# Sliding attention and dropless experts on one core: routing steps, weight sums and the first tiles' transposes put in another order

## The chip, the cores and the metric

The kernel runs on one NeuronCore of a Trainium2 chip. The metric is the device time of one execution in microseconds; the time before is 662.97 us, the median of three runs (662.25 to 666.29).

## The reference

The attention has 8 batches, 8 heads, 576 positions and head dimension 64, with an ALiBi bias and a causal window of 128. Its output, 4608 rows of 512, goes to a layer of 8 experts (512 to 1024 to 512): each row goes to the expert with the greatest logit and is weighted with that expert's probability.

```python
scores = scale * np.matmul(q, k.transpose(0, 1, 3, 2))
scores = np.where(mask, scores + bias[None], -1000000000.0)
attn = np.exp(scores - np.max(scores, axis=-1, keepdims=True))
attn = attn / (np.sum(attn, axis=-1, keepdims=True) + 1e-09)
x = (attn @ v).transpose(0, 2, 1, 3).reshape(B * S, H * D)

logits = x @ w_gate
expert_idx = np.argmax(logits, axis=1)
gate_w = softmax(logits)[np.arange(N), expert_idx]
h = np.maximum(x_sorted[lo:hi] @ w1[e], 0.0)     # per expert e
y_sorted[lo:hi] = h @ w2[e]
return gate_w[:, None] * y_sorted[inv_perm]
```

## The kernel before

The order of the work is written by hand: every engine gets its instructions in the order in which the program's text is run, and works them off in that order.

**Attention.** Two batches make a pair, and there are four pairs (bp 0 to 3). A unit is a pair and two heads, so there are 16 units, four to a pair. The loop over i (64 steps) goes through the units in four steps each (g 0 to 3). A unit's work is: scores for four groups of key blocks (L792, TensorE or PE), their exponentials on ScalarE (ACT, L801 and L811), a multiplication with the bias factors on VectorE (DVE, L805, called the probability multiply below), the products with v (values, L835), the sums of the probabilities (L874) that DVE adds up (L886), and copies of the output into xT (L854, L856). Scores run three or four groups ahead of the values.

**Routing.** When a pair's fourth unit is done, `behind(bp)` returns 16 lists of routing steps (ten for pair 2), and `some()` runs one list in each of the following steps of the loop: in g 0, 1 and 3 behind the step's values, in g 2 between the sums and the next scores. The steps are:

- `gate` (L894 on PE, L899 and L901 on DVE): logits and sums of the pair, in three parts; `turn` (L918, copied by ACT at L919) turns them into gsr
- `scale_a`, `scale_a2`, `scale_b`, `scale_b2`: L927 to L979 on DVE, from gsr to the logits, their maximum and the choice of expert
- `scale_c`: the exponential (L984, ACT), then L986 to L990 on DVE, whose last product is es, the scales of the rows; `count` is L996
- `scales_squared` (L1134): four matmuls that read es; ACT copies them to sq (L1142)
- `place` (L1005 and L1007 on PE, then L1009 to L1022), `place2` (L1028 to L1037), `ones_at` (L1046, L1052), `ones_at2` (L1061), `enlist` (L1071 on PE)
- rows of pair 0: `squares_turned` (rt, a DVE transpose, L1156), then ro: `squares_scaled` (a copy of sq, L1164, POOL) and `squares_out` (four stores on POOL's queue for a whole tile, L1175)
- rows of pairs 1 and 2: `row_turned` (four transposes on PE, L1105, and a copy by ACT, L1107), then `row_out` (a copy of es and the store, POOL, L1114 and L1119); `row` (rs) is both

In pair 2 `early_holes` (L1238 on PE, L1240 to L1242 on DVE) stands ahead of enlist. The gates, turns, head sums, row transposes and small products all take their output banks from one pool of two, `ps_m`, so each waits until the bank of the one before the last has been read.

**Queues.** SP's queue holds the loads of q, k and v for two units ahead; each waits, by a read of one probability (`no_earlier_than`), for the multiply of the next step. POOL's queue holds the stores of the rows and later the gathers.

**Weight sums.** The experts use Strassen's scheme with seven half-size products, for which sums of quarters of w1 are made on DVE (L533 to L536, eight additions of 128x512 for expert 0, `ws_tasks`). They are spread over the steps i = 48, 49, 54, 55, 58, 59, 62 and 63, ahead of the step's `some()`.

**First tiles.** Behind the attention, expert 0's four gathered tiles are scaled (L1364), turned (`to_columns`, L1378) and copied (L1379). The first two turns stand between the three gates of pair 3: turn, gate, turn, gate, gate. The experts' matmuls (`strassen1`, L1601, and `strassen2`, L1668) use six banks of their own, `pair(0)` to `pair(2)`; in their order pair 2 is needed from the fourth product on.

Of the kernel before, what the change touches and what calls it, by code (L numbers as in the profile page):

```python
# [8 lines left out]
F32 = mybir.dt.float32  # L9
# [7 lines left out]
P = 128  # L17
# [441 lines left out]
def kernel(  # L459
# [50 lines left out]
    with ExitStack() as fast:  # L510
# [377 lines left out]
        def gate(bp, c):  # L888
            if bp not in gs:
                gs[bp] = xp.tile([P, 2 * S], F32, name="gs", bufs=1)  # L890
            ps = ps_m.tile([P, 512], F32, name="m")
            c0, n = ((0, LQ), (LQ, LQ), (2 * LQ, P))[c]
            for hp in range(HP):
                nc.tensor.matmul(  # L894
                    ps[32 * hp : 32 * hp + 32, :n], lhsT=wgd[:, hp, :], rhs=xT[bp][:, hp, c0 : c0 + n],
                    start=True, stop=True,
                )
            if c < 2:
                nc.vector.tensor_tensor(gs[bp][:, c0 : c0 + n], ps[:, :n], sumT[bp][:, :LQ], op=ALU.add)  # L899
            else:  # L900
                nc.vector.tensor_tensor(  # L901
                    gs[bp][:, c0 : c0 + n].rearrange("p (b q) -> p b q", b=2),
                    ps[:, :n].rearrange("p (b q) -> p b q", b=2),
                    sumT[bp][:, None, LQ:].to_broadcast([P, 2, S - LQ]), op=ALU.add,
                )
# [460 lines left out]
        def to_columns(g, j):  # L1366
            n = g["n"]
            nm = "" if n == NJ else "1"
            if j == 0:
                g["xT"] = g["pool"].tile([P, DB, n * P], F32, name="xgT" + nm)  # L1370
            c0, m = (j // 2 * g["half"] + j % 2 * P, min(P, g["half"] - j % 2 * P)) if n == NJ else (0, P)
            to = g["xT"][:, :, c0 : c0 + m]
            xn = g["xn", j]
            if in_rows(g):
                xn = xn.rearrange("p h a f -> p (h a f)")
                tp = ps_m.tile([P, 512], F32, name="m")
                for db in range(DB):
                    nc.tensor.transpose(tp[:, db * P : (db + 1) * P], xn[:, db * P : (db + 1) * P], ident[:])  # L1378
                nc.scalar.copy(to, tp.rearrange("p (d q) -> p d q", d=DB)[:, :, :m])  # L1379
            else:  # L1380
                m = parts_of(g)
                nc.vector.transpose(to[:, :, : m * TQ].rearrange("p h (k j) -> p k h j", j=TQ), xn[:, :m])  # L1382
# [40 lines left out]
        def behind(bp):  # L1423

            g3 = [lambda k=k: gate(bp, k) for k in range(3)]
            t3 = [lambda k=k: turn(bp, k) for k in range(3)]
            rs = [lambda t=t: row(bp, t) for t in range(TPB)]
            a, a2, b, b2, c, n, q, p, p2, o, o2, e = (
                [lambda f=f: f(bp)] for f in (
                    scale_a, scale_a2, scale_b, scale_b2, scale_c, count, scales_squared, place, place2, ones_at,  # L1430
                    ones_at2, enlist,
                )
            )
            if bp == 0:
                rt = [lambda t=t: squares_turned(bp, t) for t in range(TPB)]
                ro = [
                    lambda t=t: (squares_scaled(bp, t), squares_out(bp, t, nc.gpsimd)) for t in range(TPB)
                ]
                return [g3[0:1], g3[1:2], g3[2:] + t3[0:1] + rt[0:1], t3[1:] + rt[1:3], a, a2, b, b2, c + n, rt[3:5],
                        q + p, p2 + rt[5:6] + ro[0:2], o + ro[2:4], o2 + ro[4:5], rt[6:8] + ro[5:7],  # L1440
                        e + rt[8:9] + ro[7:9]]
            rt, ro = ([lambda t=t, f=f: f(bp, t) for t in range(TPB)] for f in (row_turned, row_out))
            if bp == 1:
                return [g3[0:1], g3[1:2], g3[2:] + t3[0:1], t3[1:], a + rt[0:1], a2 + rt[1:2], b + rt[2:3],
                        b2 + rt[3:4], c + n, rt[4:5], p + ro[0:2], p2 + ro[2:5], o + rs[5:6], o2 + rs[6:7], rs[7:8],
                        e + rs[8:9]]
            return [g3, t3, a + a2, b + b2 + rt[0:1], c + n + rt[1:2], rt[2:4] + ro[0:2], p + p2 + ro[2:4] + rt[4:6],
                    o + o2 + ro[4:6] + rt[6:8], ro[6:8] + rs[8:9] + [early_holes], e + [early_table, lambda: gather(fixed[0], x_d[: 3 * 2 * S, :])]]

# [2 lines left out]
        def some():  # L1452
            if tasks:
                for f in tasks.pop(0):
                    f()
# [15 lines left out]
        for i in range(NG):  # L1471
# [30 lines left out]
            else:  # L1502
                values(u, 1, (6, 7, 8))
                finish(u, 1)
            if i in (48, 49, 54, 55, 58, 59, 62, 63):
                ws_tasks.pop(0)()
            if u == len(units) - 1 and g == 1:
                first = [t for _, t in prepare(fixed[0])]
                tasks.extend([[], first[0] + first[1][1:]])
            if g != 2:  # L1510
                some()
            if g in (1, 3):
                scores_to(ahead)
            if g == 3 and hp == HP - 1 and bp < BP - 1:
# [318 lines left out]
        while tasks:  # L1833
            some()
        g_of = [lambda k=k: gate(BP - 1, k) for k in range(3)]
        for f in first[1][:1] + g_of[:1] + first[2] + g_of[1:]:
            f()
        for i in range(len(groups)):
# [78 lines left out]
```

## Time and profile before

| what | us |
|---|---|
| runs, median (lowest to highest) | 662.97 (662.25 to 666.29) |
| the profiled execution, time of its own | 661.93 |
| its span, first to last instruction | 660.1 |
| TensorE busy | 630.1 |
| weight load busy (lies beside the matmuls) | 527.8 |
| VectorE busy | 366.1 |
| GpSimd (POOL) busy | 271.5 |
| ScalarE busy | 214.9 |

All times in rows are microseconds from the start of the span. A row of the order of time has the start, the length (of several instructions that follow each other, from the first start to the last end), the engine, the line, the operation with its tiles, the count, and in brackets the time for which the engine was idle before it and what ended that. The attention with its routing fills the first 163 us; the experts follow. Pair 0 is routed from some 45 to 83 us, pair 1 from 82 to 121, pair 2 from 123 to 153.

### The profile page before, as it was taken

The numbers are of one execution on the slowest core, as the hardware profiler recorded it, in microseconds if no ns is written. First come the engines' busy times: TensorE is split into PE (matmuls) and PEld (weight loads), VectorE is DVE, ScalarE is ACT, GpSimd is POOL, SyncE is SP. The second block draws the span as 40 slices with busy tenths as digits, with TensorE's granted clock in tenths as the row PEclk, the third lists the DMA queues.
The fourth block names the chain that finished last, engine by engine and source line by source line (L and its number), as shares of the span: only waits on it lengthen the run. The fifth ranks groups of instructions, "written<-read, shape, count | busy, mean of one in ns | idle before, by whom it ended". The sixth has DMA issues, their size and how long they took to land.

```text
span 660.1 us, 14485 instructions
## 1 busy us (share of the span) xinstructions
PE 630.1 (95%) x5824; PEld 527.8 (80%) x5824; DVE 366.1 (55%) x745; ACT 214.9 (33%) x493; POOL 271.5 (41%) x459
## 2 busy tenths in 40 slices
PE   6889999998999999999999999999999999999993
PEld 5768877687987888878878887889788978887883
DVE  3437968588798758436633761484247435643510
ACT  6858677585330331023002311320131123102310
POOL 8100664234032783566066525642662466030002
PEclk9999999999999999999999999999999999999998
DMA  9885999975258924673196419443924592376002
GB/s 265 246 214 146 254 282 284 329 245 151 95 134 302 347 57 148 218 290 90 74 306 210 153 46 312 159 149 114 322 90 143 188 303 44 127 244 224 0 1 74
DMA packets 54928, 121.81 MB, mean 185 GB/s; under 512 B 5777, under 2 KB 21297, under 8 KB 54850
## 3 DMA queue, kind: packets, MB, share of 16 engines
q1 hardware_dynamic: 43074, 92.51, 44.0%
q0 software_dynamic: 10624, 27.38, 13.1%
q8 instruction: 48, 0.79, 0.5%
q10 hardware_dynamic: 1152, 0.88, 0.4%
q14 instruction: 30, 0.25, 0.1%
HBM read 101.58 MB, written 19.63 MB: 184 GB/s over the span
## 4 chain that ended last, share of the span: by engine, by line
PE 57%; issue 9%; DVE 7%; POOL 1%; ACT 0%; POOLq 0%; DVEq 0%
PE pair0a L1668 4%; PE pair1b L1668 4%; PE pair1a L1668 4%; PE pair0b L1668 4%; PE pair1a L1601 4%; PE pair1b L1601 4%; PE pair0b L1601 4%; PE pair2b L1668 4%; PE pair2a L1668 4%; PE pair0a L1601 4%; PE pair2b L1601 3%; PE pair2a L1601 3%; PE pair0a L1726 2%; PE pair2a L1726 2%; PE pair0a L1709 1%
## 5 line engine op out<-in xcount | busy, mean ns | idle before, releaser
L1345 POOL DMA_INDIRECT xg<-x_rows,p_idx x121 | 128.3, 1061 | 33.7 <-issue 28.0
L1693 POOL DMA_INDIRECT out_dram<-zo,s_idx x38 | 43.4, 1141 | 173.3 <-DVE zo L1682 144.8
L805 DVE TENSOR_TENSOR pe<-pe,fac 128x512 f32<-128x512 f32 x64 | 43.6, 688 | 41.6 <-ACT pe L801 41.6
L792 PE MATMUL sp<-q_sb,k_sb 64*64 64x192 f32 (+2 forms) x1152 | 55.7, 320 | 7.8 <-DMA q_sb<-in_qT_dram 5.3
L835 PE MATMUL at<-pe,v_sb 64*64 64x192 f32 (+2 forms) x1408 | 55.1, 282 | 2.5 <-issue 1.4
L835 PEld LDWEIGHTS at<-pe,v_sb 64*64 64x64 f32 x1408 | 47.2, 134 | 8.5 <-issue 2.8
L792 PEld LDWEIGHTS sp<-q_sb,k_sb 64*64 64x64 f32 x1152 | 40.4, 136 | 16.5 <-issue 6.6
L801 ACT ACTIVATE pe<-sp 128x512 f32<-128x512 f32 x64 | 38.4, 599 | 30.2 <-issue 14.2
L811 ACT ACTIVATE pe<-sp,mid 128x128 f32<-128x128 f32 x128 | 40.0, 371 | 0.0
L1615 ACT ACTIVATE h<-h 128x512 f32<-128x512 f32 (+1 forms) x32 | 20.0, 624 | 38.9 <-DVE h L1614 38.9
L874 PE MATMUL m<-pe,ind 128*32 128x192 f32 (+2 forms) x576 | 25.6, 311 | 1.7 <-issue 1.0
L1543 POOL COPY paced_by<-h 1x1 f32<-1x1 f32 x47 | 18.5, 393 | 19.6 <-DVE h L1717 15.8
L1364 DVE TENSOR_TENSOR xn<-xg 128x512 f32<-128x512 f32 (+1 forms) x39 | 25.7, 662 | 1.3 <-DMA xg<-x_rows,p_idx 1.3
L874 PEld LDWEIGHTS m<-pe,ind 128*32 128x32 f32 x576 | 19.0, 109 | 6.7 <-issue 1.4
L1164 POOL COPY xs<-sq 128x16 f32<-128x16 f32 x6 | 1.7, 290 | 51.3 <-ACT sq L1142 51.3
L541 DVE TENSOR_TENSOR w2s<-w 128x512 f32<-128x512 f32 x16 | 10.9, 684 | 20.6 <-DMA w<-in_moe_w_dram 20.6
L1382 DVE STREAM_TRANSPOSE xgT<-xn 128x512 f32<-128x512 f32 (+1 forms) x31 | 21.7, 698 | 1.1
L854 ACT COPY xT<-at 128x640 f32<-128x640 f32 (+1 forms) x32 | 18.9, 591 | 5.8 <-PE at L835 5.7
L1175 POOL DMA_DIRECT2D x_rows<-xs x32 | 17.3, 553 | 7.8 <-DVE h L1614 2.3
L1668 PE MATMUL pair1a<-w,h 128*128 128x256 f32 x72 | 17.1, 380 | 0.0
L1668 PE MATMUL pair1b<-w,h 128*128 128x256 f32 (+1 forms) x72 | 17.0, 379 | 0.0
L1601 PE MATMUL pair0a<-xgT,w 128*128 128x256 f32 (+1 forms) x72 | 16.7, 375 | 0.0
(411 smaller groups left out, 1397.2 us busy)
## 6 DMA issues: line engine op xcount, KB each, us to landing
w<-in_moe_w_dram SPq DMA_DIRECT2D x29, 2048.0 KB, 8.9
k_sb<-in_kT_dram SPq DMA_DIRECT2D x15, 576.0 KB, 7.4
q_sb<-in_qT_dram SPq DMA_DIRECT2D x15, 576.0 KB, 6.6
v_sb<-in_v_dram SPq DMA_DIRECT2D x14, 320.0 KB, 4.6
v_sb<-in_v_dram SPq DMA_DIRECT2D x14, 256.0 KB, 5.0
x_rows<-xs POOLq DMA_DIRECT2D x9, 264.0 KB, 5.2
x_rows<-xT SPq DMA_DIRECT2D x8, 264.0 KB, 5.9
w<-in_moe_w_dram SPq DMA_DIRECT2D x4, 512.0 KB, 10.1
```

Of the source, the lines that this page charges most:

```text
L792: nc.tensor.matmul(by_distance(sp[c * KB : (c + 1) * KB, r, :GC], kb, 0, n), lhsT=k_sb[u][hs, c, kb * KB : (kb + 1) * KB], rhs=q_sb[u][hs, ...
L801: nc.scalar.activation(outer, sp[:, :, :GC].rearrange("p r (j x) -> p r j x", j=3)[:, :, 0:3:2, :], AF.Exp, scale=SCALE,)
L805: nc.vector.tensor_tensor(outer, outer, fac[:, h0 : h0 + 2, : 2 * w].rearrange("p r (j x) -> p r j x", j=2)[:, :, :, : 2 * KB], op=ALU.mult,)
L811: nc.scalar.activation(pe[:, r, inner], sp[:, r, inner], AF.Exp, bias=mid[:, h0 + r : h0 + r + 1], scale=SCALE,)
L835: nc.tensor.matmul(acc[r * D : (r + 1) * D, c, lo - q0 : hi - q0].rearrange("p (j x) -> p j x", x=KB), lhsT=v_sb[u // 2][c * KB : (c + 1) ...
L874: nc.tensor.matmul(sm[32 * j : 32 * j + 32, lo - q0 : hi - q0].rearrange("p (j x) -> p j x", x=KB), lhsT=ind[:, hp, :], rhs=by_distance(pe ...
L1345: nc.gpsimd.indirect_dma_start(out=to, out_offset=None, in_=where, in_offset=bass.IndirectOffsetOnAxis(ap=idx, axis=0),)
L1364: nc.vector.tensor_tensor(xn[:, :m], x, s.unsqueeze(3).to_broadcast([P, m, HP, TQ]), op=ALU.mult)
L1601: nc.tensor.matmul(ps[:, f * n : (f + 1) * n], lhsT=left[m][:, d, fb * P : (fb + 1) * P], rhs=right[m][:, d, :], start=(m in (1, 2, 5) and ...
L1668: nc.tensor.matmul(ps, lhsT=left[m][:, f, c * P : c * P + q], rhs=right[m][:, f, :], start=(m in (1, 2, 5) and f == 0), stop=True, skip_gr ...
L1693: ins = nc.gpsimd.indirect_dma_start(out=out[:, :], out_offset=bass.IndirectOffsetOnAxis(ap=s_idx[:n, g["c0"] + j : g["c0"] + j + 1], axis=0),
L1726: nc.tensor.matmul(ps[:], lhsT=g["h"][:, fb, :], rhs=g["w2"][:, fb, :], start=(fb == 0), stop=(fb == FB - 1),)
```

## The change

It alters the order of instructions and, at one place, the output bank; no instruction is added or taken away.

```diff
-                tp = ps_m.tile([P, 512], F32, name="m")
+                tp = g["banks"].pop(0) if g.get("banks") else ps_m.tile([P, 512], F32, name="m")
...
-                return [g3[0:1], g3[1:2], g3[2:] + t3[0:1] + rt[0:1], t3[1:] + rt[1:3], a, a2, b, b2, c + n, rt[3:5],
-                        q + p, p2 + rt[5:6] + ro[0:2], o + ro[2:4], o2 + ro[4:5], rt[6:8] + ro[5:7],
-                        e + rt[8:9] + ro[7:9]]
+                return [g3[0:1], g3[1:2], g3[2:] + t3[0:1] + rt[0:1], t3[1:] + rt[1:3], a + a2, b + b2, c + n + q,
+                        rt[3:4] + p + ro[0:1], rt[4:5] + p2 + ro[1:2], o + ro[2:3], o2 + ro[3:4], rt[5:6] + ro[4:5],
+                        rt[6:7] + e + ro[5:6], rt[7:8] + ro[6:7], rt[8:9] + ro[7:8], ro[8:9]]
...
-                return [g3[0:1], g3[1:2], g3[2:] + t3[0:1], t3[1:], a + rt[0:1], a2 + rt[1:2], b + rt[2:3],
-                        b2 + rt[3:4], c + n, rt[4:5], p + ro[0:2], p2 + ro[2:5], o + rs[5:6], o2 + rs[6:7], rs[7:8],
-                        e + rs[8:9]]
+                return [g3[0:1], g3[1:2], g3[2:] + t3[0:1], t3[1:], a + a2 + rt[0:1], b + b2 + rt[1:2],
+                        c + n + rt[2:3], rt[3:4] + ro[0:1], rt[4:5] + ro[1:2], p + ro[2:3], p2 + ro[3:4], o + ro[4:5],
+                        o2 + rs[5:6], rs[6:7], e + rs[7:8], rs[8:9]]
...
-            if i in (48, 49, 54, 55, 58, 59, 62, 63):
+            if i in (58, 59, 62, 63):
                 ws_tasks.pop(0)()
...
             if g != 2:
                 some()
+            if i == 49:
+                for _ in range(4):
+                    ws_tasks.pop(0)()
...
         g_of = [lambda k=k: gate(BP - 1, k) for k in range(3)]
+        fixed[0]["banks"] = pair(2)
```

The first list is pair 0's, the second pair 1's; a and a2 are scale_a and scale_a2, b and b2 scale_b and scale_b2, c scale_c, n count, q scales_squared, p place, o and o2 ones_at and ones_at2, e enlist. Pair 2's list is as it was; in its steps four of the eight weight sums now stand together behind the turns of i = 49. The banks of the first two turned tiles are those of pair 2. The program's later lines move down by three or four (L1601 is L1604 in the new text, L1668 is L1671).

Where the steps of pair 0 now stand on PE: the head sums of the sixth unit (L874, the second unit after pair 0). Before, scores follow them.

```order
L874 MATMUL m<-pe,ind 32x192 x14
L874 MATMUL m<-pe,ind 32x128 x2
L874 MATMUL m<-pe,ind 32x64 x2
L792 MATMUL sp<-q_sb,k_sb 64x3x64 x8
L835 MATMUL at<-pe,v_sb 64x64 x4
```

Now the matmuls of scales_squared stand between, and place's first matmul comes half a unit later.

```order
L874 MATMUL m<-pe,ind 32x192 x14
L874 MATMUL m<-pe,ind 32x128 x2
L874 MATMUL m<-pe,ind 32x64 x2
L1134 MATMUL m<-es,to_squares 128x72 x4
L792 MATMUL sp<-q_sb,k_sb 64x3x64 x8
L835 MATMUL at<-pe,v_sb 64x64 x4
L835 MATMUL at<-pe,v_sb 64x128 x4
L835 MATMUL at<-pe,v_sb 64x192 x8
L835 MATMUL at<-pe,v_sb 64x128 x4
L835 MATMUL at<-pe,v_sb 64x64 x4
L1005 MATMUL m<-pre,lt_strict 128x8
```

L1134 has moved ahead by one unit, past 36 score matmuls, 44 of the values and 18 of the sums, to the place right behind the sums of the step in which es is made.

On DVE in the same stretch (pr, lg, lmax, ex, sc and mx are small tiles of the routing), one piece of the difference:

```order
 L948 TENSOR_TENSOR pr<-gsr,r 128x9x32 x2
-L805 TENSOR_TENSOR pe<-pe,fac 128x2x2x128
-L886 TENSOR_TENSOR sumT<-m,sumT 64x384
-L886 TENSOR_TENSOR sumT<-m,sumT 64x320
 L957 TENSOR_TENSOR pr<-pr 128x9x32
 L958 TENSOR_TENSOR pr<-pr 128x9x16
 L959 TENSOR_TENSOR lg<-pr 128x72
 L961 TENSOR_REDUCE lmax<-lg 128x9
-L805 TENSOR_TENSOR pe<-pe,fac 128x2x2x128
 L968 TENSOR_TENSOR ex<-lg,lmax 128x72
 L972 TENSOR_TENSOR sc<-lg,lmax 128x72
```

A probability multiply and the addition of head sums stood between scale_a2 and scale_b, and a multiply between scale_b and scale_b2; now the four steps follow each other, and one multiply and the addition come behind scale_b2, ahead of scale_c.

On DVE in the first steps of pair 2 (ws is the tile of weight sums, w is w1): before,

```order
L805 TENSOR_TENSOR pe<-pe,fac 128x2x2x128 x2
L533 TENSOR_TENSOR ws<-w_2064 128x512
L899 TENSOR_TENSOR gs<-m,sumT 128x512 x2
L901 TENSOR_TENSOR gs<-m,sumT 128x128
L534 TENSOR_TENSOR ws<-ws,w_2064 128x512
```

and now:

```order
L805 TENSOR_TENSOR pe<-pe,fac 128x2x2x128 x3
L899 TENSOR_TENSOR gs<-m,sumT 128x512 x2
L901 TENSOR_TENSOR gs<-m,sumT 128x128
L533 TENSOR_TENSOR ws<-w_2075 128x512
L534 TENSOR_TENSOR ws<-ws,w_2075 128x512
L535 TENSOR_TENSOR w_2075<-w_2075 128x512
L536 TENSOR_TENSOR ws<-w_2075,ws 128x512
```

The first weight sum has moved from ahead of the gate additions to behind all three, and the third and fourth come from two units later.

## Prediction

> **What bounds the kernel now.** I read the page first, then the table of windows, then the order of time on VectorE (DVE) and TensorE (PE) in the stretches whose code changes. Sums are made on the profiled execution (span 660.1 us).
>
> ```profile
> span 660.1 us, 14485 instructions
> ...
> 60.00:70.00 10.00, 9.00 (x224) 7.47 (x216) 9.59 (x27) 6.87 (x20) 0.00 (x0) 1.00 0.64 182
> 70.00:80.00 10.00, 9.63 (x267) 8.88 (x268) 9.62 (x25) 7.06 (x21) 8.25 (x17) 1.00 0.97 276
> ```
>
> The columns are the stretch, its length, then the busy time of PE, weight load, DVE, ACT and POOL, and the granted clock. From 60 to 80 us, where pair 0 is routed, PE is busy 9.0 and 9.6 of 10 us and DVE 9.6 of 10: two engines are nearly full, and PE, which later stages need without a break, sets the end. What a moved step is worth is therefore the time for which PE waits there, and DVE has no room to do routing earlier.
>
> **Pair 0: the shorter chain.** These are DVE's rows of the routing of pair 0.
>
> ```profile
> 58.95 0.53 DVE L927 TENSOR_TENSOR s<-gsr 128x32 f32<-128x32 f32 x4
> ...
> 61.53 0.68 DVE L805 TENSOR_TENSOR pe<-pe,fac 128x512 f32<-128x512 f32 x1
> 62.13 1.05 DVE L886 TENSOR_TENSOR sumT<-m,sumT 64x384 f32<-64x384 f32 x2
> 63.22 0.46 DVE L957 TENSOR_TENSOR pr<-pr 128x288 f32<-128x288 f32 x1
> ...
> 64.47 0.68 DVE L805 TENSOR_TENSOR pe<-pe,fac 128x512 f32<-128x512 f32 x1
> 65.06 0.23 DVE L968 TENSOR_TENSOR ex<-lg,lmax 128x72 f32<-128x72 f32 x1
> ...
> 66.15 1.28 DVE L805 TENSOR_TENSOR pe<-pe,fac 128x512 f32<-128x512 f32 x2
> 67.35 0.22 DVE L986 TENSOR_REDUCE gw<-ex 128x9 f32<-128x72 f32 x1
> ...
> 68.07 0.23 DVE L990 TENSOR_TENSOR es<-r,gw 128x72 f32<-128x72 f32 x1
> ...
> 68.43 0.69 DVE L1156 STREAM_TRANSPOSE xg<-xT 128x512 f32<-128x512 f32 x1
> 69.04 0.67 DVE L1156 STREAM_TRANSPOSE xs<-xT 128x512 f32<-128x512 f32 x1
> ...
> 71.41 0.17 DVE L1009 TENSOR_TENSOR cn<-m,off 128x8 f32<-128x8 f32 x1
> ...
> 78.95 0.68 DVE L805 TENSOR_TENSOR pe<-pe,fac 128x512 f32<-128x512 f32 x1
> ```
>
> And these are PE's, of the same stretch.
>
> ```profile
> 59.14 1.51 PE L874 MATMUL m<-pe,ind 128*32 128x192 f32 x36
> 60.58 0.88 PE L792 MATMUL sp<-q_sb,k_sb 64*64 64x192 f32 x16
> ...
> 65.20 0.77 PE L835 MATMUL at<-pe,v_sb 64*64 64x192 f32 x16 [0.46 <-DVE pe L805]
> ...
> 66.89 0.34 PE L835 MATMUL at<-pe,v_sb 64*64 64x64 f32 x8 [0.26 <-DVE pe L805]
> ...
> 68.61 1.11 PE L1134 MATMUL m<-es,to_squares 128*128 128x72 f32 x8
> 70.37 0.39 PE L1005 MATMUL m<-pre,lt_strict 128*128 128x8 f32 x2 [0.65 <-ACT sq L1142]
> ...
> 77.53 0.88 PE L792 MATMUL sp<-q_sb,k_sb 64*64 64x192 f32 x16
> ...
> 82.42 1.07 PE L894 MATMUL m<-xT,wgd 128*32 128x512 f32 x8
> ```
>
> The change puts scales_squared (L1134) into the step of scale_c, right behind the head sums (L874) that start at 59.14. It reads es, the last product of scale_c. Everything on DVE up to scale_a keeps its place, so scale_a starts at 58.95 as before. From there, start to start: scale_a and scale_a2 2.58 (58.95 to 61.53), scale_b 1.25 (63.22 to 64.47), scale_b2 1.09 (65.06 to 66.15), one probability multiply 0.60 (61.53 to 62.13), the head sums' addition 1.09 (62.13 to 63.22), scale_c 0.95 (67.35 to the end of L990 at 68.30). That is 7.56 us without a pause: es is there at 66.5. PE is free for L1134 at 60.58, when it now starts the next scores. **PE waits 5.9 us.** Behind L1134 on PE stand the scores, values and sums of the attention; for the scores wait ACT's exponentials, and for those DVE and, through its paced loads, SP, whose transfers run more than a unit ahead. The 1.1 us of L1134 are moved, not added.
>
> What comes back: the waits of 0.46, 0.26 and 0.65 go, since the multiplies and the scale copies are done by then, -1.4. What is late next: after L1134 (67.65) the next multiply starts 1.6 us behind its scores (below, 88.77 on PE to 90.39 on DVE), at 69.3. From there DVE needs 0.6, the 7.54 us that now lie between 71.41 and 78.95, one transpose more (0.61, 68.43 to 69.04) and one more addition (1.09), so ones_at2 is done at 79.1. PE reaches enlist after 60.58 to 68.61 less 0.72 of waits, L1005 with 0.3, and 77.53 to 82.42 less 0.5 for the enlist matmuls that sit there now: 7.3 + 0.3 + 4.4 = 12.0, at 79.65. The two meet within 0.6 us, so I add 0.3, with bounds of 0 and 1.0. Pair 0 without any effect on the clock: 5.9 - 1.4 + 0.3 = **+4.8**.
>
> ```profile
> 88.77 0.88 PE L792 MATMUL sp<-q_sb,k_sb 64*64 64x192 f32 x16
> ...
> 90.39 0.69 DVE L805 TENSOR_TENSOR pe<-pe,fac 128x512 f32<-128x512 f32 x1 [2.27 <-ACT pe L801]
> ...
> 100.46 0.68 DVE L805 TENSOR_TENSOR pe<-pe,fac 128x512 f32<-128x512 f32 x1
> ...
> 102.62 1.38 PE L835 MATMUL at<-pe,v_sb 64*64 64x192 f32 x32
> ```
>
> **The clock behind such a wait.** A wait of 5.9 us lies in none of PE's rows between the first matmul and the last, but the two ends of the run show what idleness does.
>
> ```profile
> 4.45 1.56 PE L792 MATMUL sp<-q_sb,k_sb 64*64 64x192 f32 x16 [4.45 <-DMA q_sb<-in_qT_dram]
> ...
> L792 PE MATMUL sp<-q_sb,k_sb 64*64 64x192 f32 x32 | 2.8, 530 | 0.8 <-DMA q_sb<-in_qT_dram 0.8
> ...
> L792 PE MATMUL sp<-q_sb,k_sb 64*64 64x192 f32 x8 | 0.5, 322 | 0.0
> ...
> 647.80 1.95 PE L1760 MATMUL pair1a<-w,h 128*32 128x128 f32 x64
> ...
> 650.00:655.00 5.00, 0.00 (x0) 0.00 (x0) 0.11 (x1) 0.00 (x0) 0.98 (x1) 0.98 0.26 75
> 655.00:660.00 5.00, 0.00 (x0) 0.00 (x0) 0.00 (x0) 0.00 (x0) 0.00 (x0) 0.50 0.00 2
> ```
>
> The last matmul ends at 649.75; a mean clock of 0.98 in the stretch to 655 means a fall to 0.50 at about 654.8, 5.1 us later. At the start the same scores take 530 ns each in the stretch from 6.5 to 9.2 and 322 from 9.8 to 12.2, so the slow pace lasted some 5.3 us after the first matmul at 4.45. A wait of 5.9 is longer than 5.1. I take it that the clock halves: 5.3 us at half pace lose 2.65, of which 0.4 is the time that PE would spend on late multiplies anyway: **+2.2**, with bounds of 0 (the clock holds) and 5.3 (two such stretches). The Trainium skill, page "TensorE: Matmul & The Clock Gate", section "Why this matters for your kernels", speaks against this change: no idle gap over some 3 us between bursts, since one idle window, 3.4 us by its Part 1, brings half clock. By that rule 5.9 us hold a whole window in (5.9 - 3.4) / 3.4, about 7 of 10 positions, an estimate from that page; that the only idle stretch here needed 5.1 us fits it.
>
> **Pair 0's stores and pair 1.** The stores are the same POOL issues, now one tile a step; nothing on PE waits for them and the first gather is 70 us later, so nothing, unless a transpose must wait for a buffer (bound 0.5). In pair 1 no matmul reads es. Its scale_b2 (1.09) and scale_c with count (1.08, 67.35 to 68.43 above) now come ahead of the multiply that starts at 100.46; done some 2.1 later, at 103.3, it is used in the second half of the values at 102.62, so from 103.2: +0.3 (0 to 0.6).
>
> **Pair 2 and the first tiles.** Three waits are removed.
>
> ```profile
> 125.39 0.69 DVE L533 TENSOR_TENSOR ws<-w 128x512 f32<-128x512 f32 x1 [0.55 <-DMA w<-in_moe_w_dram]
> ...
> 126.73 0.43 PE L894 MATMUL m<-xT,wgd 128*32 128x128 f32 x8 [1.18 <-DVE gs L899]
> ...
> 145.92 0.68 DVE L535 TENSOR_TENSOR w<-w 128x512 f32<-128x512 f32 x1
> ...
> 151.49 0.54 PE L1071 MATMUL m<-oc,gsr 128*128 128x96 bf16 x9 [1.09 <-DVE hole L1240]
> ...
> 165.07 1.28 PE L894 MATMUL m<-xT,wgd 128*32 128x512 f32 x16 [0.31 <-DVE gs L899]
> ```
>
> The third gate waits 1.18 for a bank that the gate addition frees; that addition stands behind a weight sum which itself waited for its transfer. With the sums behind the gates and turns it starts some 1.2 earlier: -1.1. The four sums (4 x 0.69) then run while DVE would wait for the exponentials; without that cover they would cost 2.8. Two of them (the pair at 145.92, 1.2 us) leave the way to hole, for which enlist waits 1.09: -1.0. With the first two tiles turned in the experts' banks the second gate needs no bank of the first: -0.3 of this row and 0.2 of weight loading, -0.5. Upper bounds are the waits themselves (-2.7 in all), lower bound 0.
>
> **Sum.** 4.8 + 2.2 + 0.3 - 1.1 - 1.0 - 0.5 = +4.7. On the profiled execution's 661.93 that gives 666.6; the median of the runs shown, 662.97, lies 1.0 above it and would give 667.7. I say **667.0**.
>
> **Rivals.** First, PE waits but the clock holds at 1.00: no fall is on record for less than 5.1 us, and the estimate of 5.9 has little to spare. Then +2.5: 665.0. Second, the clock stays low for longer: at half pace PE waits in bits for multiplies, and two more stretches of 5.3 us may pass before it is busy enough. Against it, only 2.8 us of busy scores were needed at the start. Price 2 x 2.65 less 1.3 under DVE's late work: +4, 671.0; it decides once half clock outlasts some 9 us. Third, on the other side, DVE is the bound from 59 to 84 and not PE, as its 9.6 of 10 speak for: then the wait costs only what DVE loses, from the end of count (66.5 + 0.2) to the next multiply at 69.3, 2.6 us, and 2.6 + 0.3 - 2.6 = +0.3 leaves 662.7, no slower than can be told. PE's 9.63 of 10 from 70 to 80 speaks against it: it has no room to catch up. That PE's wait does not arise at all would need es before 61, for which 5.5 us of DVE work would have to vanish; I give it nothing of its own.
>
> **How the numbers follow.** Wait with half clock 0.52 (667.0, its own range 665 to 669.5), wait with full clock 0.21, DVE the bound 0.15, long half clock 0.12. Range 662.4 to 670.2: it takes in the first rival, two thirds of the third and the near part of the second. A measurement of this kernel tells about 1% (6.6 us) from no change. Slower by more: most of the long half clock and 0.06 of the forecast's tail, 0.16. Faster by more would need 656.3, below every case: 0.02. Within 1%: 0.82.
>
> **What would show it.** In the changed profile L1134 of pair 0 should stand at about 66.5 with some 5.9 us idle before it, ended by DVE's es; the granted clock of the slice after it should read below full and scores there near 530 ns; pair 1's first gate should come near 89.5 (82.42 now); the waits at L894 of pair 2 and at its L1071 should be gone, and the third gate should no longer stand behind a weight sum. The prediction is wrong if PE passes L1134 without a long wait, if the gates of pair 1 come within 2 us of now, or if the clock stays at 1.00 there.

## The result, and the profile after

The change is slower: 671.38 us median of 6 runs (667.27 to 673.63) against 662.61 us of 6 runs of the kernel before, a ratio of 1.0127, 95% interval 1.0093 to 1.0161: clear of 1, though under 2%. The profiled execution took 671.0 us with a span of 669.2 (before 661.93 and 660.1). The prediction said 667.0, with a range up to 670.2.

Where the time went is read from the starts of the head sums (L874) of each unit, which stand in the timelines of both kernels, and of the first expert matmul (L1601 before, L1604 in the change, whose lines from there on are 3 higher).

| from the start of the span to | before | change | difference | added since the row above |
|---|---|---|---|---|
| head sums of unit 0 | 11.63 | 12.89 | +1.26 | +1.26 |
| head sums of unit 5 | 59.14 | 57.29 | -1.85 | -3.11 |
| head sums of unit 9 (pair 0's routing) | 96.52 | 102.65 | +6.13 | +7.98 |
| head sums of unit 11 (pair 1's routing) | 115.85 | 123.81 | +7.96 | +1.83 |
| head sums of unit 15 (gates and routing of pair 2) | 159.07 | 165.73 | +6.66 | -1.30 |
| first expert matmul | 166.28 | 175.12 | +8.84 | +2.18 |
| end of the span | 660.1 | 669.2 | +9.1 | +0.26 |

The first two rows are no work of the change: nothing up to i = 19 is moved. They are the start and two waits of the kernel before to which the profile gives no releaser (1.0 at 37.90, 1.8 at 43.66). The 1.83 at unit 11 are for the most part such a gap too, in the change (1.80 from 119.14), with half clock behind it. So the change adds 8.0 us in pair 0's units, takes 1.3 off before unit 15 and adds 2.2 at the first tiles of the experts.

TensorE in the change, from unit 5's head sums to unit 6's. The columns are start, length, engine, line, operation, operands, count, and in brackets the idle time ahead and what ended it.

```profile
57.29 1.51 PE L874 MATMUL m<-pe,ind 128*32 128x192 f32 x36
65.05 1.95 PE L1134 MATMUL m<-es,to_squares 128*128 128x72 f32 x8 [6.24 <-DVE es L990]
66.93 1.56 PE L792 MATMUL sp<-q_sb,k_sb 64*64 64x192 f32 x16
68.26 2.55 PE L835 MATMUL at<-pe,v_sb 64*64 64x64 f32 x48
...
74.49 1.51 PE L874 MATMUL m<-pe,ind 128*32 128x192 f32 x36
```

L1134 waits 6.24 us where the sum had 5.9, and DVE's es ends the wait. Behind it the rows are long: L1134 takes 1.95 in place of 1.11, the scores 1.56 in place of 0.88. From 57.29 to 74.49 are 17.20 us, 8.03 before. DVE did nearly what was worked out, without a pause: from the start of scale_a (57.10) to the end of es, the last product of scale_c (64.67 + 0.23), are 7.80 us, where the sum had 7.56.

```profile
57.10 0.53 DVE L927 TENSOR_TENSOR s<-gsr 128x32 f32<-128x32 f32 x4
...
64.67 0.23 DVE L990 TENSOR_TENSOR es<-r,gw 128x72 f32<-128x72 f32 x1
```

The granted clock by stretches (from:to, length, busy us and count of PE, its weight loads, DVE, ACT and POOL, then PEclk, DMA share and GB/s) says why the rows are long.

```profile
60.00:63.60 3.60, 0.00 (x0) 0.00 (x0) 3.35 (x12) 0.26 (x1) 0.00 (x0) 1.00 0.25 79
63.60:67.00 3.40, 1.95 (x12) 1.85 (x14) 1.38 (x6) 0.00 (x0) 0.00 (x0) 0.50 0.23 77
67.00:70.40 3.40, 3.40 (x53) 2.81 (x57) 1.17 (x2) 1.66 (x5) 2.26 (x5) 0.50 0.22 43
70.40:74.00 3.60, 3.60 (x104) 3.38 (x102) 2.48 (x10) 2.59 (x8) 3.01 (x8) 1.00 0.82 201
```

TensorE has half its clock from 63.6 to 70.4. It works from 65.05, so 5.35 us pass at half pace and 2.7 us of work are lost.

The waits of pair 2 did go. The three gates are one row without a pause, 2.36 us long (before 3.53 from 123.63 to 127.16), and L1071 of unit 13 has no wait ahead of it (1.09 before).

```profile
132.60 2.36 PE L894 MATMUL m<-xT,wgd 128*32 128x512 f32 x24
...
158.13 0.56 PE L1071 MATMUL m<-oc,gsr 128*128 128x96 bf16 x9
```

One wait is new in this stretch, and it comes from pair 1's list:

```profile
127.21 0.63 PE L1105 MATMUL m<-ident,xT 128*128 128x128 f32 x4 [0.82 <-DVE sumT L886]
```

Enlist (L1071) now stands right behind unit 11's head sums, so both banks of the small pool are taken, and the row transpose behind it waits until DVE has added the sums. This wait of 0.81 or 0.82 us stands in all ten profiles with the new list for pair 1 and in none of the seven with the old one. It is why the row for unit 15 shows 1.3 us less and not the 2.3 of the two waits.

But the first tiles, which waited 0.43 and 0.31 before, now wait at three of their turns. TensorE of the change:

```profile
165.73 1.54 PE L874 MATMUL m<-pe,ind 128*32 128x192 f32 x36
...
169.58 0.63 PE L1378 MATMUL pair2a<-ident,xn 128*128 128x128 f32 x4 [0.83 <-ACT xT L856]
...
172.84 0.66 PE L1378 MATMUL pair2b<-ident,xn 128*128 128x128 f32 x4 [1.63 <-DVE xn L1364]
...
175.12 1.78 PE L1604 MATMUL pair0a<-xgT,w 128*128 128x224 f32 x8
177.23 0.66 PE L1378 MATMUL m<-ident,xn 128*128 128x128 f32 x4 [0.33 <-DVE gs L899]
```

The first turn's 0.83 is the price of its new bank, which is free when ACT has copied the attention's last output (L856): it is 0.74 to 0.83 in ten of the eleven kernels that have these banks. DVE's L1364, for which the second turn waits, waits for the gathered rows; so the question is what the transfers did. POOL issues the last two stores of pair 2's rows and the four gathers, SP the 2 MB load of the first expert's second weights:

```profile
158.68 1.08 POOL L1119 DMA_DIRECT2D x_rows<-xs  x2 [0.67 <-ACT xs L1107]
164.85 1.36 POOL L1345 DMA_INDIRECT xg<-x_rows,g_idx  x1 [5.09 <-DVE ws L534]
166.51 0.98 POOL L1345 DMA_INDIRECT xg<-x_rows,g_idx  x1 [0.30 <-issue]
167.80 0.95 POOL L1345 DMA_INDIRECT xg<-x_rows,g_idx  x1 [0.30 <-issue]
169.05 1.20 POOL L1345 DMA_INDIRECT xg<-x_rows,g_idx  x1 [0.30 <-issue]
```

```profile
167.46 0.39 SPq L569 DMA_DIRECT2D w<-in_moe_w_dram  x1
```

```profile
172.09 0.69 DVE L1364 TENSOR_TENSOR xn<-xg 128x512 f32<-128x512 f32 x1 [2.65 <-DMA xg<-x_rows,g_idx]
```

In the kernel before, the same issues:

```profile
150.87 1.08 POOL L1119 DMA_DIRECT2D x_rows<-xs  x2 [0.66 <-ACT xs L1107]
154.95 1.05 POOL L1345 DMA_INDIRECT xg<-x_rows,g_idx  x1 [2.99 <-DVE pe L805]
...
159.04 1.39 POOL L1345 DMA_INDIRECT xg<-x_rows,g_idx  x1 [0.30 <-issue]
```

```profile
160.80 0.39 SPq L569 DMA_DIRECT2D w<-in_moe_w_dram  x1
```

The load starts 1.73 us behind unit 15's head sums in both (160.80 - 159.07, 167.46 - 165.73): it follows TensorE. The gathers don't follow TensorE: the last one was issued at those head sums before (159.04) and 3.3 us after them now. So the load now comes ahead of two of the four, and the view of this tile gives 3.9 to 8.0 us from issue to landing, 4.2 to 5.2 before.

The first gather waits for the last store to land; the DVE rows that the profile names as its releasers had ended before. That splits the 3.3 us. From the issue of the last store (151.41 before, 159.21 now) to the head sums TensorE takes 7.66 us before and 6.52 now: 1.1 are TensorE's, which no longer waits at L1071. From that issue to the first gather are 3.54 us before and 5.64 now: 2.1 are the store's, which landed 2.56 us after its issue before and 4.66 now. The last section has what the traces show of that.

### The profile page after: what moved, and what is told of

Its sections match the earlier page's. It is cut to its first block, busy times and chain, and to the rows that moved or that the text cites. A ratio compares the mean times of both kernels' runs of the same rounds, so it can differ in the third digit from the quotient of the medians.

```text
span 669.2 us, 14485 instructions
## 1 busy us (share of the span) xinstructions
PE 635.4 (95%) x5824; PEld 530.9 (79%) x5824; DVE 366.7 (55%) x745; ACT 215.1 (32%) x493; POOL 270.9 (40%) x459
## 4 chain that ended last, share of the span: by engine, by line
PE 74%; issue 10%; DVE 9%; DMA 3%; POOL 1%; ACT 1%; ACTq 0%; POOLq 0%; DVEq 0%
PE sp L792 6%; PE at L835 6%; PE pair0a L1671 4%; PE pair1b L1671 4%; PE pair1a L1671 4%; PE pair0b L1671 4%; PE pair1a L1604 4%; PE pair1b L1604 4%; PE pair0b L1604 4%; PE pair2b L1671 4%; PE pair2a L1671 4%; PE pair2b L1604 3%; PE pair2a L1604 3%; PE pair0a L1604 3%; PE m L874 3%
## 5 line engine op out<-in xcount | busy, mean ns | idle before, releaser
L835 PE MATMUL at<-pe,v_sb 64*64 64x192 f32 (+2 forms) x1408 | 57.1, 290 | 2.7 <-issue 2.3
L1364 DVE TENSOR_TENSOR xn<-xg 128x512 f32<-128x512 f32 (+1 forms) x39 | 25.8, 664 | 5.4 <-DMA xg<-x_rows,g_idx 4.2
L874 PE MATMUL m<-pe,ind 128*32 128x192 f32 (+2 forms) x576 | 25.9, 316 | 0.7 <-DVE pe L805 0.7
L874 PEld LDWEIGHTS m<-pe,ind 128*32 128x32 f32 x576 | 19.3, 111 | 5.8 <-ACT pe L811 1.4
L1671 PE MATMUL pair1a<-w,h 128*128 128x256 f32 x72 | 17.1, 380 | 0.0
L1671 PE MATMUL pair1b<-w,h 128*128 128x256 f32 (+1 forms) x72 | 17.0, 379 | 0.0
L1604 PE MATMUL pair0a<-xgT,w 128*128 128x256 f32 (+1 forms) x72 | 16.7, 375 | 0.0
```

Of the source, the lines that this page charges most:

```text
L835: nc.tensor.matmul(acc[r * D : (r + 1) * D, c, lo - q0 : hi - q0].rearrange("p (j x) -> p j x", x=KB), lhsT=v_sb[u // 2][c * KB : (c + 1) ...
L874: nc.tensor.matmul(sm[32 * j : 32 * j + 32, lo - q0 : hi - q0].rearrange("p (j x) -> p j x", x=KB), lhsT=ind[:, hp, :], rhs=by_distance(pe ...
L1364: nc.vector.tensor_tensor(xn[:, :m], x, s.unsqueeze(3).to_broadcast([P, m, HP, TQ]), op=ALU.mult)
L1604: nc.tensor.matmul(ps[:, f * n : (f + 1) * n], lhsT=left[m][:, d, fb * P : (fb + 1) * P], rhs=right[m][:, d, :], start=(m in (1, 2, 5) and ...
L1671: nc.tensor.matmul(ps, lhsT=left[m][:, f, c * P : c * P + q], rhs=right[m][:, f, :], start=(m in (1, 2, 5) and f == 0), stop=True, skip_gr ...
```

## Experiments

All are timed against the kernel before on their own chip; what is compared is the recorded ratio, with its 95% interval (it is not quite the quotient of the medians). The kernel before had medians of 667.23 (e1 to e4), 663.63 (e5 to e8), 663.70 (e9 to e12) and 666.87 us (e13 to e15); 1% is 6.6 to 6.7 us.

| run | what it is | ratio | interval |
|---|---|---|---|
| e1 | change, L1134 and place two steps later | 1.0017 | 0.9980 to 1.0055 |
| e2 | change, L1134 alone two steps later | 1.0056 | 1.0025 to 1.0087 |
| e3 | change, 7 products ahead of L1134, both its calls | 1.0137 | 1.0088 to 1.0186 |
| e4 | before, with sums moved and banks | 0.9953 | 0.9916 to 0.9991 |
| e5 | change, 7 products, pair 0 alone | 1.0145 | 1.0106 to 1.0184 |
| e6 | the change | 1.0139 | 1.0102 to 1.0176 |
| e7 | before, with pair 0's list | 1.0122 | 1.0079 to 1.0165 |
| e8 | before, with pair 1's list | 1.0067 | 1.0038 to 1.0096 |
| e9 | change, 6 products, pair 0 alone | 1.0104 | 1.0060 to 1.0149 |
| e10 | change, 2 MB load held | 1.0090 | 1.0053 to 1.0127 |
| e11 | change without pair 0's list | 1.0048 | 1.0013 to 1.0083 |
| e12 | before, with sums moved | 1.0008 | 0.9976 to 1.0040 |
| e13 | before, with sums moved, load held | 0.9954 | 0.9921 to 0.9986 |
| e14 | before, with sums moved, banks, load held | 0.9947 | 0.9914 to 0.9980 |
| e15 | before, load held | 0.9994 | 0.9958 to 1.0030 |

### Pair 0: the wait moved, shortened, and taken alone (e1, e2, e6, e7)

e1 and e2 edit the change's list, e7 puts that list alone into the kernel before.

```diff
 # e1
-    a + a2, b + b2, c + n + q, rt[3:4] + p + ro[0:1], rt[4:5] + p2 + ro[1:2], o + ro[2:3], ...
+    a + a2, b + b2, c + n, rt[3:4], rt[4:5] + q + p, p2 + ro[0:1], o + ro[1:2], ...
 # e2
-    c + n + q, rt[3:4] + p + ro[0:1], rt[4:5] + p2 + ro[1:2],
+    c + n, rt[3:4] + p, rt[4:5] + q + p2 + ro[0:2],
```

> The change with scales_squared and place both two steps later (the step rt[4:5] + q + p), the squares' stores a step later for it; a + a2, b + b2 and all other parts stay. Theory (the wait for es and the half clock behind it are the loss): in the profile of the change es is done at 64.90 and PE, without the wait, reaches the new place of L1134 about 5.6 us after the head sums that start at 57.29, at 62.9, so a wait of about 2 us is left in place of 6.24, too short to fill a window; clock 1.00 from 58 to 90; of the 8.0 us that pair 0 costs some 6 come back: 665 to 666. Rival (the price lies in the other parts of the change, pair 1 and the tail, or DVE is the bound from 58 to 84 whatever PE waits for): 669 or more.

> The change with scales_squared alone two steps later, ro[0:1] with it; place stays one step behind scale_c. Theory: the next matmul that needs DVE's chain, L1005 of place (it reads pre, done at 65.1), now stands where PE arrives at about 60.8; the wait moves there and shrinks to about 4.3 us, so 1.9 come back, and the half clock may stay or go by where the gap lies: 667 to 669.5. Rival (L1134's own place is the whole cause): no wait over 1 us at L1005 and 663 to 664.

> The change itself, for its time beside the parts on one chip: 1.0127 times the kernel before, 8 to 9 us, as in the first measurement; its span differs by where instruction gaps fall, its wait at pair 0's L1134 (6.2) and the two windows of half clock behind it stay.

> The kernel before with the change's list for pair 0 alone. Theory: this list holds the whole loss, 8.0 us by the distances between head sums in the profile of the change: the change's excess over before, plus what the tail's parts give back (3.1 in its run): 8 to 11 us over before on the same chip. Rival (the loss is spread over the lists and the tail): 5 or less.

TensorE of e1, then of e2:

```profile
64.30 1.08 PE L1134 MATMUL m<-es,to_squares 128*128 128x72 f32 x8 [0.76 <-DVE es L990]
...
75.22 0.56 PE L1071 MATMUL m<-oc,gsr 128*128 128x96 bf16 x9 [1.99 <-DVE gsr L1061]
```

```profile
66.68 0.56 PE L1005 MATMUL m<-pre,lt_strict 128*128 128x8 f32 x2 [4.34 <-DVE pre L996]
```

In e1 the wait at L1134 is 0.76 (2 were expected; scores ahead of it already waited 1.17 for a buffer), and in e2 the wait moves to L1005, 4.34 where 4.3 was expected. So it is not that one matmul: the list asks TensorE to wait for DVE's whole chain within a step or two. From unit 5's head sums to unit 9's, 37.4 us before and 45.4 in the change, e1 takes 41.9 (56.54 to 98.41) and e2 42.5 (58.70 to 101.22): 3.5 and 2.8 of the 8.0 come back, not 6 and 1.9. In e1 the next price shows: L1071, come earlier, waits 1.99 for DVE, and half clock follows that wait too. The ratios fall by more than that, and this part is not pair 0's: in both profiles the 2 MB load is issued behind the last gather (165.53 against 163.28, 170.69 against 168.99), and no tile is late.

e7 settles that pair 0's list alone is a loss of this size: it costs 1.22%, 8.1 us (interval 5.2 to 11.0), and its units took 8.0 us longer in the profile of the change. Its own profile has the same wait, 6.25 us, and the same 6.83 us of half clock. e6 gives the change 1.39% on that chip.

### The clock behind the wait (e3, e5, e9)

The wait stays, but TensorE is kept busy in it: products of the identity go into the bank that L1134 then overwrites.

```diff
 def scales_squared(bp):
     ...
+    for _ in range(7):                      # e3;  7 if bp == 0 else 0: e5;  6 if bp == 0 else 0: e9
+        nc.tensor.matmul(ps[:], lhsT=ident[:], rhs=xT[bp][:, 0, :512], start=True, stop=True)
```

> The change with seven more 128x512 products of the identity in front of L1134, into the same bank, which L1134 then overwrites: PE is busy for about 5.3 of the 6.24 us that it waits, at the same place, and everything else stays. Theory (the half clock is half work lost): the granted clock stays at 1.00 from 60 to 72, L1134 takes 1.1 in place of 1.95 and the work up to 70.4 runs at full pace: 2.7 less, 668.7. Rival (DVE bounds the stretch, so a slower PE costs nothing there): the clock stays full and the time is the change's, 671 to 671.5.

> As the filled kernel, but the seven products stand in front of L1134 for pair 0 alone. The filled kernel also had them in front of the same function's matmuls for the last pair, at 198.96 among the experts, where they cost 6.2 less 1.2, 5.0 us on a PE without gaps; in its profile the clock stayed at 1.00 and the stretch from unit 5's head sums to unit 6's took 14.64 in place of the change's 17.20. Theory (half clock is lost work): 2.6 less than the change on the same chip. Rival (what is won there is waited for later): the same as the change.

> The change with six 128x512 products in front of pair 0's L1134 alone (seven took 6.28 us, just past the wait, and added 56 rows to TensorE's program). Its profile: clock 1.00 from 56 to 90, units 5 to 6 in 14.6 us in place of 17.2. Theory (half clock is lost work, and the run with seven products missed its 2.6 by where other gaps fell): 1.0105 times before, 2.6 less than the change's 1.013 to 1.014. Rival (it is won at unit 6 and waited for later, so the clock behind the wait costs the end nothing): 1.013 to 1.015.

e3 does not answer the question: the function is called for the last pair too, among the experts, and there the products cost 5.0 us of a TensorE without gaps. e5 and e9 leave that call alone. TensorE of e9 (its lines are 2 higher), and its clock:

```profile
59.69 5.42 PE L1134 MATMUL m<-xT,ident 128*128 128x512 f32 x12
66.00 1.08 PE L1136 MATMUL m<-es,to_squares 128*128 128x72 f32 x8 [0.90 <-DVE es L990]
...
72.89 1.51 PE L874 MATMUL m<-pe,ind 128*32 128x192 f32 x36
```

```profile
60.00:64.00 4.00, 4.00 (x10) 1.71 (x9) 3.72 (x13) 0.28 (x2) 0.00 (x0) 1.00 0.43 150
64.00:68.00 4.00, 3.10 (x43) 2.10 (x45) 1.93 (x7) 0.55 (x2) 0.17 (x1) 1.00 0.22 66
```

The clock stays at 1.00, L1136 takes 1.08, and units 5 to 6 take 14.64 us (72.89 - 58.25, the row of its head sums) in place of 17.20: the half clock costs 2.6 us here. All three filled kernels show 14.64 or 14.65. The whole time of e9 agrees (1.0104 against 1.0127 and 1.0139), that of e5 doesn't: in e5's profile the third tile waits 3.52 us under the 2 MB load. The stage settles the price; the totals alone would not, their intervals overlap. The mean granted clock reaches beyond the profiled executions: its median is 0.989 in 27 executions of the kernels that wait idly there (the change, e6, e7, e10; 0.984 to 0.992) and 0.994 in the 12 of e5 and e9 (0.989 to 0.996).

### Pair 1 alone, and all but pair 0 (e8, e11)

e8 puts the change's list for pair 1 into the kernel before; e11 puts the old list for pair 0 back into the change. The lines of both are in the diff of the change.

> The kernel before with the change's list for pair 1 alone. Theory (the prediction's +0.3, bounds 0 to 0.6): no difference that can be measured; the 1.8 us by which units 9 to 11 took longer in the profile of the change come from one longer instruction gap (2.04 at 118.91 against 0.99 at 112.97) and a window of half clock behind it, which another execution won't show at that place. Rival (the list itself costs it): +1.8 and waits for DVE at its routing matmuls in the profile.

> The change with pair 0's list as before. Theory (pair 0's list is the whole loss; pair 1's list costs nothing once the weight sums no longer stand ahead of the third gate): as the tail's parts alone, 0.995 to 0.998 times before. Rival (the 4.4 us of pair 1's list alone stay): 1.002 or more, with its price at units 9 to 12.

e8 is slower by 0.67% where nothing was expected. DVE and TensorE at its pair 2's gates:

```profile
131.65 0.69 DVE L533 TENSOR_TENSOR ws<-w 128x512 f32<-128x512 f32 x1 [1.90 <-DMA w<-in_moe_w_dram]
```

```profile
132.99 0.54 PE L894 MATMUL m<-xT,wgd 128*32 128x128 f32 x8 [2.53 <-DVE gs L899]
```

From unit 11's head sums to unit 15's it takes 47.32 us, 43.22 before. The row transpose waits its 0.81. The weight sum that stands ahead of the gate additions now waits 1.90 for its transfer (0.55 before), the third gate 2.53 (1.18 before), and the clock is at half for 3.42 us from 133.16. In the change the sums no longer stand there, so that this part of the price is e8's own, and the row transpose's 0.8 is what the list itself costs. From unit 9 to unit 11, where the forecast had its 0.3, the list costs nothing that can be told: in none of the ten profiles with it does TensorE wait there for anything that has a releaser, and without the gaps that have none the distance is 17.80 to 18.64 us with the old list and 17.97 to 18.39 with the new one (three profiles with half clock there left out).

e11 refutes "0.995 to 0.998": without pair 0's list the change is still slower by 0.48%, interval 0.13 to 0.83. Its gates and its L1071 have no waits, but the row transpose waits 0.81 and the third tile 1.70, by way of DVE's L1364, which waits 2.75 for the third gather: the load is issued at 163.26, the last two gathers at 163.25 and 164.50. These two waits less the 2.3 us that went make 0.2 us, under the interval's 0.9, so that a part of e11's loss stays unexplained. The load has its own experiments.

### The tail: what was won, and what took it (e4, e10, e12 to e15)

e4 and e12 are the diff's own lines on the kernel before. The held load is one line:

```diff
+        no_earlier_than(fixed[0]["xg"][0:1, NJ - 1, 0, 0:1])
         load_w2(fixed[0], w2_a)
```

> The kernel before with the last two parts of the change alone: four weight sums behind the gates and turns of the step of i = 49, and the first two tiles turned in the experts' banks. Theory (the prediction's terms): the waits of 1.18 at the third gate and 1.09 at L1071 go, and 0.5 at the first tiles: 2.6 less than before, 660.0. Rival (the 2.2 us that the profile of the change loses between the last head sums and the first expert come from these parts): 664 to 665.

> The kernel before with the four weight sums moved, alone. Theory: the third gate's wait on a sum that waits for its transfer and the wait at L1071 of unit 13 go, 2.3 less, minus what the first tiles then wait for their gather: 0.995 to 0.998 times before. Rival (the banks gave the tail's parts their 3.1): 1.000.

> The change with one small transfer ahead of the 2 MB load of the first expert's second weights on SP, reading the last of the four gathered tiles, so that the load starts when all four have landed. In the profiles of the change the load is issued 1.73 us behind unit 15's head sums, ahead of the last gathers; the tiles that land under it take 7.3 to 9.3 us from issue in place of 4 to 5, and PE waits 2.1 to 3.5 us for one of them. Theory (this collision is a loss of its own): all tiles land in about 4 to 5 us, no wait over 1 us at the first four turns, 2 less than the change: 1.010 to 1.011. Rival (the gather is late by itself, since its rows land late): the waits stay, or the load is late for the expert, and the time is the change's.

> The kernel before with the four weight sums moved and the 2 MB load held until the last gathered tile has landed. Theory (the sums' move saves 2.3 and the load that overtakes the gathers takes it back): no wait over 1.5 us at the first four turns, 0.996 to 0.997 times before. Rival (the sums' move saves nothing on the path): 1.000.

> As the run before it, with the first two tiles in the experts' banks too: both parts of the change's tail, the load held. Theory: as the sums' move alone with the load held, within 0.5 us, 0.996 to 0.997; the banks trade a wait for a sum for one for ACT's last copy. Rival (the banks save the 0.5 of the prediction and more): 0.994 or less.

> The kernel before with the 2 MB load held until the last gathered tile has landed, and nothing else. Theory (in its profile the load is issued at 160.80, behind the last gather at 159.04, and no turn waits over 0.5): no difference, 1.000. Rival (the load is late or early for something else, so that holding it changes the time by itself): off 1.000 by more than 0.003.

e12, the moved sums alone, gains nothing (1.0008), against the expected 0.995 to 0.998. In its profile unit 15's head sums start at 156.49, 2.6 ahead of before, and then the load is issued behind only two of the gathers. POOL, SP and TensorE of e12:

```profile
157.26 0.98 POOL L1345 DMA_INDIRECT xg<-x_rows,g_idx  x1 [0.30 <-issue]
```

```profile
158.21 0.39 SPq L569 DMA_DIRECT2D w<-in_moe_w_dram  x1
```

```profile
160.25 0.66 PE L1378 MATMUL m<-ident,xn 128*128 128x128 f32 x4 [0.74 <-DVE xn L1364]
...
164.08 0.64 PE L1378 MATMUL m<-ident,xn 128*128 128x128 f32 x4 [2.19 <-DVE xn L1364]
165.92 2.36 PE L894 MATMUL m<-xT,wgd 128*32 128x512 f32 x16 [1.19 <-DVE gs L899]
```

The turns and gates wait 0.74, 2.19 and 1.19, the gates run at half clock (2.36 for 16), and the first expert starts at 168.21, 1.9 later than before.

e10 holds the load in the change. SP and TensorE of e10:

```profile
177.41 0.57 SPq L646 DMA_DIRECT2D pace<-xg  x1
178.22 0.39 SPq L569 DMA_DIRECT2D w<-in_moe_w_dram  x1
```

```profile
174.21 0.65 PE L1378 MATMUL pair2a<-ident,xn 128*128 128x128 f32 x4 [0.79 <-ACT xT L856]
...
175.79 0.66 PE L1378 MATMUL pair2b<-ident,xn 128*128 128x128 f32 x4
...
179.20 0.60 PE L1378 MATMUL m<-ident,xn 128*128 128x128 f32 x4
```

No turn waits for a gather any more, and the change goes from 1.0127 and 1.0139 to 1.0090, with intervals that overlap. With the load held, the moved sums gain what they should (e13, 0.9954); the load held in the kernel before changes nothing (e15, 0.9994), since there it came behind the gathers anyway. So the moved sums are a gain (0.9 to 5.3 us by e13's interval), and the profiles of e12 and the change show the load that overtakes the gathers taking it back. By the times alone its share is not settled: the intervals of e12 and e13 just overlap, and they ran on two chips. The banks add nothing that can be told (e14 against e13): the 0.31 of the gate's wait goes, and the first turn's 0.8 comes. e4 had shown 0.9953 without the held load; in its profile unit 15's head sums take 4.3 us in place of 1.5, in short gaps to which the profile gives no releaser, the load falls behind the gathers (163.08 against 160.62), and no tile is late. The single profiles of e13 and e14 have such gaps too (4.1 and 3.8 us), so that the gain stands in their times and not in the distances of those profiles.

e14 is faster than the kernel before, and by its ratio than the change: 0.9947, interval 0.9914 to 0.9980, a median of 663.94 against 666.87 us on its chip.

## Why the prediction was wrong

**Pair 0, +4.8 and +2.2.** Right in mechanism and nearly in size: 8.0 in place of 7.0. The wait was 6.24 for 5.9. The half clock lasted 6.83 us (two stretches of 3.41), not 5.3, of which TensorE worked 5.35: 2.6 to 2.7 for the 2.2. Its scores took 538 ns each, and pair 1's first gate came at 88.06, 5.6 later than before and 7.5 later counted from unit 5's head sums. The rest of the 1.0, some 0.2, is in what should have come back. The Trainium skill, page "TensorE: Matmul & The Clock Gate", section "Why this matters for your kernels", spoke against a gap of over 3 us, and this one agrees.

**Pair 1, +0.3.** Another wait than the one forecast. The values behind unit 9, for which it expected a late multiply, wait for nothing; the price is the 0.8 at a row transpose behind unit 11, where enlist took the second bank.

**Pair 2, -1.1 and -1.0.** Both waits went, 1.2 and 1.1 us, as forecast.

**The first tiles, -0.5: the step that failed.** It took the turns and gates there to be bound by banks and sums. They are bound by the gather, which waits for the last store of pair 2 to land and not for TensorE, while the 2 MB load follows TensorE. The forecast moved TensorE ahead by 2.1 us and left both transfers where they were; it named the waits that go and not what is late next. Of its 2.1 only the 1.1 at L1071 come between the last store and the head sums; the other 2.1 us of the collision are the store's own lateness, for which the forecast had nothing. Measured, the tiles take 2.2 more: -2.6 in the sum became about 0 (-1.2 - 1.1 + 2.2). The bank's -0.5 is a part of that: its wait was traded for another.

The terms as measured, 8.0 + 0.8 - 0.1, give 8.7; the time says 8.8 (671.38 - 662.61, with an interval of some 2 us to either side, so that the close fit is in part luck). The 4.0 that the sum was short are 1.0 of pair 0, 0.5 of pair 1 and 2.5 of the tail.

**The rivals.** That the clock holds is refuted by the profile, that DVE is the bound and the wait costs nothing by e7 (8.1 us) and by e1. The long half clock named 671.0, very near, but for another reason: it asked for half clock beyond some 9 us, and that lasted 6.83. A right time from a wrong cause; no case joined a half clock as forecast with a tail that gains nothing.

## What to carry to other kernels

A matmul that is moved ahead of its operand costs the wait and, in a stream that has no room to catch up, the half clock behind it: here 6.2 and 2.6 us, and the second could be measured by filling the wait with products that nobody reads. A wait that is removed moves one engine against transfers that do not follow it: ask of each transfer near the place what starts it, and which two change their order. A bulk load that nothing reads for 25 us (issued at 167.46 in the change, first read at 192.47) is best held behind the small transfers that the next matmul waits for; that line cost nothing that can be told (e15) and kept 2.5 to 3.6 us by the ratios of e10 and e13, whose intervals overlap those beside them.

## What the runs showed of the hardware

**When the clock halves.** Between 20 us and the last matmul, the half clock came in lengths of 3.41 to 3.42 or 6.82 to 6.83 us in every profile that has it, whatever the gap. Its starts lie on a grid: in e3 they are at 41.04, 122.96, 140.03 and 174.16, which is 24, 5 and 10 steps of 3.413 us, and in every profile with more than one start they are whole steps apart. The Trainium skill, page "TensorE: Matmul & The Clock Gate", Part 1, has a free-running window of 3.4 us, and that agrees. But the bound of some 3 us of idleness in that page's section "Why this matters for your kernels" does not hold here: 1.80 us were enough in the change,

```profile
120.94 0.44 PE L835 MATMUL at<-pe,v_sb 64*64 64x128 f32 x6 [1.80 <-issue]
```

```profile
120.00:122.00 2.00, 1.05 (x10) 0.66 (x9) 0.46 (x1) 0.00 (x0) 0.55 (x2) 0.91 1.05 348
122.00:124.00 2.00, 2.00 (x29) 1.48 (x32) 0.00 (x0) 0.80 (x2) 0.61 (x2) 0.50 1.11 258
124.00:126.00 2.00, 2.00 (x40) 1.35 (x35) 0.69 (x1) 1.48 (x4) 0.13 (x1) 0.74 1.06 392
```

while the kernel before had a gap as long with the clock at 1.00 all through:

```profile
43.50:45.50 2.00, 0.17 (x8) 0.03 (x3) 0.69 (x1) 0.75 (x3) 0.00 (x0) 1.00 0.70 163
45.50:47.00 1.50, 1.50 (x28) 0.91 (x29) 0.45 (x1) 1.08 (x3) 0.00 (x0) 1.00 0.83 252
```

What differs is where the gap falls on the grid. The step of the grid that holds the gap had TensorE busy for 0.47 of its length in the change (118.22 to 121.64, where the clock halves), and for 0.52 in the kernel before (43.84 to 47.25). Over all 17 profiles, from 9 to 640 us, every step at full clock with a busy share of 0.47 or less (14 of them) was followed by half clock, and none with more than 0.69; between the two, three were and most were not. No run was made to move a gap along the grid, so this is what the traces fit and not a tested rule.

**Small transfers beside a large one.** A gathered tile landed 4.2 to 5.2 us after its issue before; with the 2 MB load between, the slowest took 8.0 (the change), 7.9 (e6) and 9.3 us (e5). The Trainium skill, page "DMA: Bandwidth & Descriptors", section "Queues, rings and completion order", says that each transfer engine takes its queues in turn; the trace agrees in that the small transfers are stretched and not put behind the whole load: in the change the two late tiles landed at 175.78 and 177.09, the load's last packet at 178.80.

**Packets of the instruction queue.** The trace names a queue "instruction", with packets of 16 KB. In the thirteen kernels with the moved sums, 15 of the last store's 16 shares had landed 2.5 to 2.6 us after its issue, as all 16 had in the four others, and the last share 1.1 to 2.1 us later. In each of the thirteen such a packet ran just then, and the store's next packet began within 0.02 us of its end (161.14 to 162.79 and 162.78 in the change); in the four others that packet began after the landing (154.11 against 153.97 before). The gaps of TensorE without a releaser, which came at the same few places of the program in most profiles (near 16, 28, 34, 38 and 43 us, and in unit 11), bear a like mark: all 32 of over 0.9 us between 10 and 170 us ended 1.0 to 1.7 us after such a packet did, which about one moment in eight would do by chance. Those of over 0.45 us add up to between 1.1 and 7.0 us in one profile. So a changed order of instructions may reach the transfers and the gaps by way of this queue; no run moved such a packet by itself, and the cause is not shown.
